# Local-global attention and a gated feed-forward on one core: the order of all steps as a written table, scores one pair of heads a stage

## The chip, the cores and the metric

The kernel runs on one core of a Trainium2 chip. The metric is device time in microseconds (us) of one execution. The core's engines each work through their own queue in order: TensorE (PE in the profile, its weight loads PEld), VectorE (DVE), ScalarE (ACT), GpSimd (POOL), and the sync engine (SP), whose queue here issues all loads and stores. An instruction whose inputs are not ready holds everything behind it in its queue.

## The reference, cut to what matters

```python
# batch 8, 8 heads, 512 local and 32 global positions, head size 64
k_all, v_all = concat(k_g, k_l), concat(v_g, v_l)
out_g = softmax(q_g @ k_all.T / 8) @ v_all                   # global rows see everything
s_ll = where(|i - j| <= 32, q_l @ k_l.T / 8, -1e9)           # local rows: a band of 32 ...
out_l = softmax(concat(q_l @ k_g.T / 8, s_ll)) @ v_all       # ... and the global keys
x = concat(out_g, out_l) with the heads side by side         # (8, 544, 512)
h = relu(x @ w_in)                                           # 512 -> 1024
c = conv over positions, three taps, each channel by itself, with conv_w
out = (h * sigmoid(c)) @ w_out                               # 1024 -> 512
```

The three weights of the feed-forward arrive as float64.

## The kernel before, in words

Everything is cut into short steps, named by a key and a number, and each step sends a few instructions to one engine.

*Attention.* Heads are taken in pairs (n = 0, 2, ..., 62; eight heads a batch). LQ, LK, LV and LG load queries, keys, values and global queries. S multiplies one pair's queries with its keys (64 small matmuls, L337) into one of two PSUM tiles, `four[0]` and `four[1]`. M (L370, DVE) adds the band mask and takes the minimum, E (L380, ACT) exponentiates with a sum, NS (L387, L388, DVE) inverts the sum, NP multiplies with it (L394 on ACT, L401 on POOL), DT (L409, DVE) transposes in blocks of 32. For four heads together, P (L433, 160 small matmuls) multiplies with the values into both `four` tiles. G, GM (L480), GE (L489), GN (L496, L497) and GS (L510 on POOL, L512 on DVE) do the same for the global rows; XG (L470) and GX (L518, a copy, L520) collect their outputs. XH0, XH1 (copies, ACT) and XL0, XL1 (L461, DVE) split the local outputs into a high and a low part, the tile `x`.

*Feed-forward.* A unit u is 128 of the 1024 hidden channels for one batch, eight units a batch (u = 0 to 63), and u = 64 to 71 for the global rows of all batches. Za and Zb (six matmuls of 512 columns each, L545) make it, RE is the relu (L558 on ACT), C1 (L321), Ca and Cb (L572, DVE) are the three taps; for two units together TH (L579, ACT) is the tanh of the sigmoid, GG (L583, DVE) the gate, GH (copy, ACT) and GL (L285) the high and low part. Oa to Od (six matmuls each, L603) make 128 of the 512 outputs of a batch (o = 0 to 35), OE copies them out, ST stores. Za needs both XL0 steps of its batch and Zb both XL1 steps, so the units of a batch start when both its P steps have been split.

*Weights.* WD loads one of eight pieces. WA (L145), WB (L150), WC (L155, L158), WH, WL (L161, L246), and WS and WX rebuild high and low parts from the float64 bits; i = 0 to 3 are `w_in`, 4 to 7 `w_out`. WT does the same for the taps (L150 to L195).

*The order.* A planner (`plan`, `arranged`) simulates the five engines with a table of costs and a due time for each step (POS, POS0, POS1, POS7), starts on each engine the ready step with the earliest due time, and the start times give the order in which `emit` writes the steps; instructions of one engine are then tied to that order. Which engine a step with a choice uses is set for batch 0 (`ENG0`), batch 1 (`ENG1`) and the rest (`ENG`):

```python
ENG = dict(XH0="a", XH1="a", XC="p", GC="a", GS="v", GX="v", NP="a", RE="a", C1="p", GH="a", GL="v", OE="v")
ENG1 = dict(ENG, OE="a")
ENG0 = dict(ENG, NP="p", GL="p", OE="a", GS="p", WA="a", WH="a", WX="a")
```

("a" is ACT, "v" DVE, "p" POOL.) From batch 1 on the scores of two pairs are one step (`JOINED_S = 1`): 128 matmuls, into both `four` tiles. Buffers that bound the order: four PSUM banks for Z, O and weight sums, the two `four` tiles, three query tiles, two value tiles, two `hb` tiles (relu output of two units each), two output tiles.

The steps on PE stand in this order at the start of before: WS.0 S.0 WS.1 S.2 S.4 WS.3 G.0 S.6 P.0 S.8(+10) G.8 P.4 Za.0 S.12(+14) WS.2 Zb.0 Za.1 P.8 Zb.1 Za.2. On DVE: WT.0 WC.0 WL.0 WC.1 WL.1 M.0 M.1 WC.3 NS.0 WL.3 M.2 M.3 M.4 M.5 NS.2 WC.6 GM.0 GM.1 NS.4 GN.0 GN.1 M.6 M.7 DT.0 DT.2 DT.1 DT.3 NS.6 DT.4 WL.6 XG.0 XL0.0 XL1.0 DT.5 DT.6 DT.7 M.8 M.9 M.10 WC.4 NS.8 M.11 WL.4 GM.2 GM.3 NS.10 GN.2 GS.8 GN.3 DT.8 XG.4 GX.0 WC.2 XL0.4 XL1.4 WL.2. The sequence of PE steps goes 72 times from the large matmuls (Z, O, WS) to the small ones (S, G, P) or back.

Of the kernel before, what the change touches and what calls it, by code (L numbers as in the profile page):

```python
# [52 lines left out]

# [10 lines left out]

# [3 lines left out]


def joined(n, since):  # L70

    return n // H >= since


def group(n, since):

    return (n // 4 * 4, n // 4 * 4 + 2) if joined(n, since) else (n,)
# [7 lines left out]
def attn_moe(ctx: ExitStack, tc: tile.TileContext, q_d, k_d, vw_d, qg_d, w_in_d, w_out_d, cw_d, out_d):  # L85
# [23 lines left out]

# [33 lines left out]
    def magnitude(w1, t):  # L143
        if ENGS[0]["WA"] == "a":
            nc.scalar.activation(out=f(t), in_=f(w1), func=AF.Abs)  # L145
        else:
            nc.vector.tensor_scalar(out=t, in0=w1, scalar1=0x7FFFFFFF, scalar2=None, op0=ALU.bitwise_and)
# [146 lines left out]


# [29 lines left out]
    def SC(n):  # L325

        for i, n in enumerate(group(n, JOINED_S)):
            q, chunk = heads[n]["q"], n // 2 % 4
# [1 line left out]
            for j in range(2):  # L330
                heads.setdefault(n + j, {})["s"] = four[side][:, j, :].rearrange("p (r x) -> p r x", r=NR)
            for r in range(NR):
                a = (5 * chunk + r) * SG
                for c in range(4):
                    for j in range(2):
                        rows = slice(j * D, (j + 1) * D)
                        nc.tensor.matmul(  # L337
                            heads[n + j]["s"][c * SG : (c + 1) * SG, r, :], lhsT=q[rows, c, r * SG : (r + 1) * SG],
                            rhs=keys[rows, c, a : a + P], start=True, stop=True,
                        )  # L340
# [297 lines left out]
LIMIT = dict(h=2, o=2)  # L638

ENG = dict(  # L640
    XH0="a", XH1="a", XC="p", GC="a", GS="v", GX="v", NP="a", RE="a", C1="p", GH="a", GL="v", OE="v",
)
ENG1 = dict(ENG, OE="a")
ENG0 = dict(ENG, NP="p", GL="p", OE="a", GS="p", WA="a", WH="a", WX="a")
ENGS = (ENG0, ENG1, ENG)

WENG = "pppppppp"

POS = dict(
    LQ=-1179.98, LK=-3410.21, LG=1302.26, LV=-1044.64, S=-1927.26, M=-1916.07, E=-935.04, NS=2891.3, NP=8253.39,  # L650
    DT=-2510.34, P=-1946.35, XH0=1800.87, XH1=-4498.84, XL0=2189.67, XL1=3093.6, XC=5534.43, G=-1339.63,
    GM=-3274.47, GE=-451.99, GS=2245.45, GN=26.63, GT=-36.81, GC=28, GR=-0.44, GP=47.15, XG=-348.91, GQ=-4.66,
    GX=5026.07, GY=-21.58, Za=1343.76, Zb=-2970.26, RE=-593.24, C1=3333.74, Ca=2145.9, Cb=-2645.65, TH=1498.45,
    GG=-2809.9, GH=-734.2, GL=-6125.32, Oa=1476.86, Ob=-1928.39, Oc=1677.17, Od=-912.14, OE=617.79, ST=951.33,
    WD=-36.77, WA=33.34, WB=-18.75, WC=6.7, WH=38.83, WL=26.89, WN=20.71, WS=61.46, WX=14.24, WT=67.84,
)
POS1 = dict(
    LQ=1801.42, LK=-2868.41, LG=-3799.69, LV=-472.71, S=2444.32, M=1149.47, E=-672.25, NS=-5513.89, NP=2844.69,
    DT=1050.29, P=-4401.47, XH0=1286.05, XH1=2015.12, XL0=-2118.02, XL1=-717.31, XC=216.22, G=-2968.21,
    GM=-6577.04, GE=-1509.99, GS=3918.06, GN=712.21, GT=-229.9, GC=0.84, GR=4.1, GP=-28.82, XG=-1414.41, GQ=-30.93,  # L660
    GX=5714.37, GY=43.7, Za=-2590.8, Zb=-4371.92, RE=3415.51, C1=-122.5, Ca=-335.52, Cb=2146.37, TH=-1163.25,
    GG=-2103.3, GH=-3088.62, GL=4104.62, Oa=-1516.5, Ob=1968.56, Oc=-140.95, Od=219.28, OE=1828.41, ST=-6497.37,
    WD=-22.76, WA=-48.75, WB=-114.27, WC=-13.6, WH=0.78, WL=36.32, WN=-36.15, WS=38.29, WX=36.81, WT=-5.41,
)
POS0 = dict(
    LQ=-16.41, LK=-2244.01, LG=-2092.66, LV=-1226.62, S=1696.13, M=-664.98, E=86.91, NS=4459.15, NP=-2141.79,
    DT=4976.67, P=1974.19, XH0=-2061.92, XH1=1997.55, XL0=998.26, XL1=1299.57, XC=-2968.56, G=-3718.28,
    GM=-2110.34, GE=-2428.29, GS=-3518.18, GN=1309.03, GT=97.28, GC=-3.17, GR=39.33, GP=23.89, XG=-1857.03,
    GQ=-22.35, GX=1016, GY=50.57, Za=-581.53, Zb=1607.5, RE=-4855.65, C1=1559.02, Ca=705.17, Cb=-2338.26, TH=-2415,
    GG=-1071.76, GH=-2120.18, GL=5170.42, Oa=-3178.86, Ob=73.19, Oc=2656.84, Od=-1298.34, OE=491.38, ST=-327.94,  # L670
    WD=78.19, WA=80.77, WB=36.03, WC=-4.08, WH=21.61, WL=52.37, WN=-25.74, WS=-1.32, WX=40.49, WT=1.93,
)

POS7 = dict(
    LQ=2645.41, LK=-880.16, LG=2823.5, LV=1027.03, S=1496.11, M=210.85, E=-1231.68, NS=2371.06, NP=-1797.04,
    DT=1559.96, P=864.56, XH0=-1384.4, XH1=632.04, XL0=302.77, XL1=-2816.76, XC=-2975, G=-2414.68, GM=-476.12,
    GE=-2919.87, GS=2467.17, GN=-2779.13, GT=-36.81, GC=28, GR=-0.44, GP=47.15, XG=4526.77, GQ=-4.66, GX=-370.08,
    GY=-21.58, Za=555.05, Zb=-2600.7, RE=4478.11, C1=3298.11, Ca=-6114.75, Cb=589.4, TH=5989.37, GG=4383.12,
    GH=204.2, GL=-2432.36, Oa=2107.51, Ob=-1249.42, Oc=-6742.44, Od=3984.32, OE=-1144.6, ST=-1401.11, WD=-36.77,
    WA=33.34, WB=-18.75, WC=6.7, WH=38.83, WL=26.89, WN=20.71, WS=61.46, WX=14.24, WT=67.84,  # L680
)

POSS = (POS0, POS1, POS, POS7)
POSS_NAMES = ("POS0", "POS1", "POS", "POS7")
PHASE = (0, 1, 2, 2, 2, 2, 2, 3, 3)

LATE = (2113.34, 2097.81, 2247.08)
WPOS = [-3504.56, -1841.02, 715.35, -15.71, 675.83, 1857.69, 482.76, 1530.63]
LAST_BATCH = 7
SUMMED = 1200, 6000  # L690

def cost(key, e, wide=True):


    def act(n, calls=1, src=190, more=0):
        one = src + n * 5 // 6 - 100 + more
        return one * calls, one * calls + 100

    def psum(n, calls=1):
        one = 150 + n * 102 // 100 - 77
        return one * calls, one * calls + 80

    def fast(n, calls=1):
        one = 150 + n * 52 // 100 - 77
        return one * calls, one * calls + 77

    def two(n):
        return 110 + n, 190 + n  # L710

    def pool2(n):
        return 150 + n * 22 // 10, 180 + n * 22 // 10

    def pool1(n, calls=1):
        return (180 + n * 107 // 100) * calls, (180 + n * 107 // 100) * calls + 30

    def pe(t, more=175):
        return t, t + more

    def dma(kb):
        return kb * 1024 // 320, kb * 1024 // 320 + 2000

    n = SL if wide else 8 * GV - 2
    if key in COPIES:
        n, from_psum = {"GH": (2 * n, 0), "OE": (n, 1)}.get(key, COPIES[key])
        if e == "a":
            return act(n, src=155 if from_psum else 190)
# [392 lines left out]
```

## Time and profile before

| what | value |
|---|---|
| device time, median of 3 runs | 536.71 us (534.94 to 536.86) |
| the profiled execution: time, span | 535.9 us, 534.1 us |
| PE busy | 491.1 us (92% of the span) |
| PEld busy | 400.6 us (75%) |
| DVE busy | 419.7 us (79%) |
| ACT busy | 333.2 us (62%) |
| POOL busy | 107.3 us (20%) |
| HBM read, written | 39.35 MB, 8.96 MB (90 GB/s over the span) |

The span runs from the first to the last instruction. Busy shares are means over the whole span, and the first 70 us and the rest behave differently, so the stretches have to be read apart.

### The profile page before, as it was taken

To read this page: it belongs to the slowest core of one execution; us is meant where nothing else is said; L and a number is where in the kernel's file an instruction comes from. 1 tells how busy PE (TensorE), PEld (TensorE's weight loads), DVE (VectorE), ACT (ScalarE), POOL (GpSimd) and SP (SyncE) were. 2 spreads that over 40 slices of the span, in tenths; PEclk is the share of its full clock that TensorE was granted. 3 is DMA by queue.
4 is the path that set the end of the run, shared out by engine and by line. 5 is a ranking of instruction groups with operands and counts; after the bars stand their busy time and mean duration, and the time that the engine had idled before them with its cause. 6 is when DMAs were issued, how large, how long until landed. Compare 5 with 4: busy or idle time off the path is not lost.

```text
span 534.1 us, 16508 instructions
## 1 busy us (share of the span) xinstructions
PE 491.1 (92%) x6752; PEld 400.6 (75%) x6752; DVE 419.7 (79%) x1263; ACT 333.2 (62%) x1016; POOL 107.3 (20%) x153
## 2 busy tenths in 40 slices
...
GB/s 334 412 311 172 170 133 130 128 114 80 120 70 100 67 111 71 112 152 52 78 95 134 70 81 92 129 71 22 70 41 22 22 21 22 20 20 41 40 37 46
DMA packets 32668, 53.56 MB, mean 100 GB/s; under 512 B 2384, under 2 KB 20304, under 8 KB 31568
## 3 DMA queue, kind: packets, MB, share of 16 engines
...
HBM read 39.35 MB, written 8.96 MB: 90 GB/s over the span
## 4 chain that ended last, share of the span: by engine, by line
PE 80%; DVE 13%; ACT 4%; issue 1%; DMA 1%; SPq 0%; DVEq 0%
PE ps_o L603 34%; PE ps_h L545 31%; PE four L433 8%; PE four L337 5%; DVE pt L370 2%; DVE t L572 2%; DVE pt L409 2%; DVE wt L158 1%; PE psw L261 1%; PE four L358 1%; DMA cwr<-cw 1%; ACT pt L380 1%; DVE pt L512 1%; DVE pg L480 1%; ACT pt L394 1%
## 5 line engine op out<-in xcount | busy, mean ns | idle before, releaser
L603 PE MATMUL ps_o<-g,w_out 128*128 128x512 f32 (+1 forms) x864 | 207.1, 380 | 0.0
L545 PE MATMUL ps_h<-x,w_in 128*128 128x512 f32 x768 | 197.9, 395 | 6.9 <-DVE x L461 4.4
L603 PEld LDWEIGHTS ps_o<-g,w_out 128*128 128x128 f32 x864 | 154.7, 188 | 31.3 <-issue 1.9
L545 PEld LDWEIGHTS ps_h<-x,w_in 128*128 128x128 f32 x768 | 142.7, 189 | 39.8 <-DVE x L461 5.1
L572 DVE SCALAR_TENSOR_TENSOR t<-hb,cw,t 128x512 f32<-128x512 f32 (+1 forms) x144 | 103.9, 741 | 32.9 <-POOL t L321 32.4
L321 POOL TENSOR_SCALAR t<-hb,cw 128x512 f32<-128x512 f32 (+1 forms) x72 | 57.8, 806 | 316.7 <-ACT hb L558 284.6
L380 ACT ACTIVATE pt<-pt,negm 128x128 f32<-128x128 f32 x256 | 99.1, 391 | 14.5 <-DVE negm L370 14.4
L558 ACT ACTIVATE hb<-ps_h 128x512 f32<-128x512 f32 (+1 forms) x72 | 41.4, 575 | 76.8 <-PE ps_h L545 71.5
L394 ACT ACTIVATE pt<-pt,sums 128x128 f32<-128x128 f32 x224 | 69.0, 400 | 1.0 <-DVE sums L387 1.0
L579 ACT ACTIVATE t<-t 128x1024 f32<-128x1024 f32 (+1 forms) x36 | 36.6, 1016 | 37.4 <-DVE t L572 37.3
L433 PE MATMUL four<-pt,vf 32*64 32x128 f32 (+3 forms) x2560 | 49.2, 295 | 10.5 <-DVE pt L409 3.8
L370 DVE CUSTOM_DVE_ANT_0 pt<-four,mask 128x128 f32<-128x128 f32 x256 | 55.6, 284 | 3.0 <-PE four L337 3.0
L433 PEld LDWEIGHTS four<-pt,vf 32*64 32x64 f32 x2560 | 44.6, 139 | 16.9 <-issue 10.4
L409 DVE STREAM_TRANSPOSE pt<-pt 128x608 f32<-128x608 f32 (+1 forms) x64 | 52.3, 853 | 1.6 <-ACT pt L394 1.6
L583 DVE SCALAR_TENSOR_TENSOR t<-t,hb 128x1024 f32<-128x1024 f32 (+1 forms) x36 | 42.2, 1174 | 12.4 <-ACT t L579 12.2
L380 ACT ACTIVATION_READ_ACCUMULATOR pt<-pt,negm 128x1 f32 x256 | 48.7, 190 | 0.0
L282 ACT CAST g<-t 128x1024 fp32r<-128x1024 f32 (+1 forms) x36 | 36.3, 1007 | 15.0 <-DVE t L583 10.9
L337 PE MATMUL four<-k,q 64*32 64x128 f32 x2048 | 37.7, 298 | 5.9 <-DVE pg L480 3.6
L285 DVE TENSOR_TENSOR g<-t,g 128x1024 fp32r<-128x1024 f32 (+1 forms) x32 | 36.9, 1154 | 6.5 <-ACT g L282 6.3
L337 PEld LDWEIGHTS four<-k,q 64*32 64x32 f32 x2048 | 32.4, 115 | 12.2 <-issue 4.1
L282 ACT CAST x<-four 128x384 fp32r<-128x384 f32 x64 | 19.4, 381 | 19.9 <-PE four L433 17.7
L282 DVE COPY o<-ps_o 128x512 f32<-128x512 f32 (+1 forms) x28 | 18.3, 654 | 14.0 <-PE ps_o L603 13.8
...
## 6 DMA issues: line engine op xcount, KB each, us to landing
vf<-vw SPq DMA_DIRECT2D x16, 640.0 KB, 4.2
q<-q SPq DMA_DIRECT2D x32, 256.0 KB, 4.0
out<-o SPq DMA_DIRECT2D x32, 256.0 KB, 2.1
...
```

Of the source, the lines that this page charges most:

```text
L282: nc.scalar.copy(out=out, in_=in_) if choice(key) == "a" else eng(key).tensor_copy(out=out, in_=in_)
L321: nc.gpsimd.tensor_scalar(out=out, in0=in_, scalar1=by, scalar2=0.0, op0=ALU.mult, op1=ALU.add)
L337: nc.tensor.matmul(heads[n + j]["s"][c * SG : (c + 1) * SG, r, :], lhsT=q[rows, c, r * SG : (r + 1) * SG], rhs=keys[rows, c, a : a + P], s ...
L370: nc.vector.tensor_tensor_reduce(out=out, in0=st["s"][:, r, :], in1=mask[:, v : v + 4].rearrange("p a c -> p (a c)"), op0=ALU.add, op1=ALU ...
L380: nc.scalar.activation(out=p, in_=p, func=AF.Exp, scale=-1.0, bias=st["m"][:, r : r + 1], accum_out=two["r"][:, n % 2, r : r + 1],)
L394: nc.scalar.activation(out=p, in_=p, func=AF.Copy, scale=by[:, r : r + 1])
L409: nc.vector.transpose(out=t, in_=t)
L433: nc.tensor.matmul(out, lhsT=vf[rows, j, s, :], rhs=pt, start=s == order[0], stop=s == order[-1])
L545: nc.tensor.matmul(hid[u]["z"], lhsT=w[:, ft, ct, :], rhs=x, start=ct + i == 0, stop=ct == NCT - 1 and i == 2)
L572: nc.vector.scalar_tensor_tensor(out=t, in0=rows_of(u, k)[:, u % 2], scalar=cw[:, 3 * ft + k : 3 * ft + k + 1], in1=t, op0=ALU.mult, op1=A ...
L583: nc.vector.scalar_tensor_tensor(out=t, in0=t, scalar=1.0, in1=rows_of(u, 1), op0=ALU.add, op1=ALU.mult)
L603: nc.tensor.matmul(ps, lhsT=w_out[w][:, mt, ft, :], rhs=g[:, k, ft % 2, :], start=ft + i == 0, stop=ft == NFT - 1 and i == 2,)
```

## The change: what it does

The planner is gone; the order is a table, `ORDER`, that `emit` walks through. Engines are set by `ENGINES`, and for single steps by `MOVED`. The scores of every pair are a step of their own, with the `four` tile given by `SIDES`. The taps' load is a step of its own (CW), their WT step is split (WTa on ACT) and two instructions shorter, and both stand later.

Counted over the table: 1471 steps for 1455 (14 more S, CW, WTa); PE goes 84 times between large and small matmuls. Steps with another engine than before: to ACT from POOL NP.1, 3, 5, 6, 7 and C1.0, 1, 3, 4, 5, 9, 10, 12, 15; to POOL from ACT NP.9, 10, 12, 13, 14; to POOL from DVE GS.8, 9, 12, 13, GX.0, GX.8, GL.9; to DVE from POOL WB.0, WB.2, GL.3, GL.7; to DVE from ACT RE.10, 11, 12 and OE.0, 1, 3, 6, 7. GL.1 and GL.5 stay on POOL.

The steps on PE at the start of after: S.0 S.2 WS.0 S.4 WS.1 G.0 S.6 WS.3 P.0 S.8 S.10 G.8 P.4 S.12 Za.0 S.14 Zb.0 WS.2 Za.1 Zb.1 Za.2 P.8. On DVE: WB.0 WC.0 WL.0 M.0 WC.1 M.2 M.1 WL.1 M.3 M.5 M.4 WC.3 NS.2 GM.0 GM.1 WL.3 NS.0 GN.1 M.7 GN.0 M.6 DT.3 DT.1 DT.2 DT.0 NS.4 WC.6 WL.6 XG.0 NS.6 XL1.0 XL0.0 DT.5 M.9 M.8 M.10 M.11 DT.7 WC.4 GM.3 DT.6 GM.2 DT.4 NS.10 WL.4 GN.3 WB.2 WC.2 XG.4 XL0.4 XL1.4 NS.8 GN.2 WT.0 WL.2. On SP: WD.0 LK.0 LG.0 LQ.0 WD.1 LQ.2 LK.2 LG.16 LK.6 LQ.6 LK.4 LQ.4 WD.3 LV.0 LV.4.

```diff
-    def rest(out, w0, w1, p, low):
-
-        v = nc.vector
-        v.tensor_scalar(out=w1, in0=w1, scalar1=low, scalar2=None, op0=ALU.bitwise_and)
-        v.scalar_tensor_tensor(out=f(w1), in0=w0, scalar=2.0**-32, in1=w1, op0=ALU.mult, op1=ALU.add)
-        v.scalar_tensor_tensor(out=out, in0=f(w1), scalar=2.0**-20, in1=f(p), op0=ALU.mult, op1=ALU.mult)
...
+    def CW(i):
+        nc.sync.dma_start(out=cwr.rearrange("p n w -> p (n w)"), in_=cw_d)
...
+    def WTa(i):
+        if wpe == 2:
+            magnitude(cwr[:, :, 1], cw.bitcast(U32))
...
-            magnitude(w1, t)
             clamped(t, nc.vector)
             scaled_bits(w1, t, 0x7FFFF8)
             power(cwp, t)
-            rest(f(cwp), w0, w1, cwp, 0)
+            nc.vector.scalar_tensor_tensor(
+                out=f(cwp), in0=w0, scalar=2.0**-52, in1=f(cwp), op0=ALU.mult, op1=ALU.mult
+            )
...
     def choice(key):
-        return ENGS[phase[0]][key]
+        for e, which in MOVED.get(key, {}).items():
+            if now[0] in which:
+                return e
+        return ENGINES[key]
...
     def SC(n):
 
-        for i, n in enumerate(group(n, JOINED_S)):
-            q, chunk = heads[n]["q"], n // 2 % 4
-            side = i if joined(n, JOINED_S) else SIDE["S", n]
+        q, chunk = heads[n]["q"], n // 2 % 4
+        for j in range(2):
+            heads.setdefault(n + j, {})["s"] = four[int(SIDES[n // 2])][:, j, :].rearrange("p (r x) -> p r x", r=NR)
...
-        nc.vector.tensor_tensor(out=t, in0=t, in1=gos[2 * b + 1], op=ALU.add)
+        eng("GX").tensor_tensor(out=t, in0=t, in1=gos[2 * b + 1], op=ALU.add)
         cp("GX", hi, t)
-        nc.vector.tensor_tensor(out=lo, in0=t, in1=f(hi), op=ALU.subtract)
+        eng("GX").tensor_tensor(out=lo, in0=t, in1=f(hi), op=ALU.subtract)
...
+MOVED = {
+    "C1": {"a": (0, 1, 3, 4, 5, 9, 10, 12, 15,)},
+    "GL": {"p": (1, 5, 9,)},
+    "GS": {"p": (0, 1, 4, 5, 8, 9, 12, 13,)},
+    "GX": {"p": (0, 8,)},
+    "NP": {"p": (0, 2, 4, 9, 10, 12, 13, 14,)},
+    "OE": {"a": (2, 4, 5,)},
+    "RE": {"v": (10, 11, 12,)},
+    "WB": {"v": (0, 2,)},
+}
...
+SIDES = "01001001010101101101101001010101"
...
+ORDER = """
+WD.0 LK.0 LG.0 LQ.0 WD.1 LQ.2 LK.2 WA.0 WB.0 LG.16 LK.6 S.0 WC.0 LQ.6 LK.4 WL.0 WH.0 LQ.4 WD.3 WA.1 LV.0 LV.4
+S.2 M.0 WB.1 WD.6 WD.2 E.0 WC.1 WS.0 M.2 WH.1 M.1 E.2 WL.1 S.4 WX.0 M.3 WA.3 WS.1 M.5 E.1 WB.3 M.4 WC.3 E.3 G.0
...
+Cb.68 Cb.69 Zb.70 TH.69 Oc.30 GG.69 GH.69 Za.71 RE.70 C1.70 Od.30 Ca.70 GL.69 Zb.71 OE.30 Od.31 Cb.70 RE.71
+C1.71 Ca.71 Oa.32 Cb.71 OE.31 TH.71 Ob.32 ST.31 GG.71 Oa.33 ST.30 GH.71 Oc.32 GL.71 Ob.33 Od.32 Oc.33 OE.32
+ST.32 Oa.34 Od.33 Ob.34 OE.33 ST.33 Oa.35 Ob.35 Oc.34 Oc.35 Od.34 Od.35 OE.34 ST.34 OE.35 ST.35
+"""
+def emit(tc, now, fns):
...
+    for step in ORDER.split():
+        key, i = step.split(".")
+        now[0] = int(i)
```

## Rows read from the trace of the kernel before

**Rows 1.** Busy time by stretch: stretch, its length, engines, PEclk, DMA share, GB/s.
```profile
6.20:68.50 62.30, 35.20 (x826) 24.18 (x827) 53.92 (x195) 45.22 (x148) 27.79 (x41) 0.79 0.83 280
68.50:140.00 71.50, 68.61 (x1127) 54.94 (x1126) 67.70 (x211) 58.18 (x186) 23.98 (x21) 0.96 0.42 113
...
140.00:482.00 342.00, 338.52 (x4504) 277.32 (x4503) 274.16 (x810) 216.61 (x662) 47.37 (x59) 1.00 0.23 71
482.00:534.10 52.10, 48.79 (x300) 44.15 (x298) 22.61 (x37) 11.14 (x19) 5.48 (x11) 1.00 0.11 42
```

**Rows 2.** Waits of PE from 82 us on: waiter, releaser, total us, times, longest.
```profile
PE ps_h L545 <- DVE x L461: 2.2, 1, 2.2
```

**Rows 3.** Timeline of PE around one joined score step: start, us, instruction group.
```profile
167.27 1.52 PE L545 MATMUL ps_h<-x,w_in 128*128 128x512 f32 x6
168.72 2.12 PE L337 MATMUL four<-k,q 64*32 64x128 f32 x128
170.76 1.66 PE L603 MATMUL ps_o<-g,w_out 128*128 128x512 f32 x6
...
173.64 1.52 PE L603 MATMUL ps_o<-g,w_out 128*128 128x512 f32 x6
```

**Rows 4.** Timeline of DVE up to the end of batch 0's `x`.
```profile
6.21 0.18 DVE L150 TENSOR_SCALAR cw<-cw 128x24 f32<-128x24 f32 x1 [2.70 <-ACT cw L145]
...
8.50 0.68 DVE L155 TENSOR_SCALAR wt<-wt 128x1024 uint32<-128x1024 uint32 x1
...
19.04 0.29 DVE L370 CUSTOM_DVE_ANT_0 pt<-four,mask 128x128 f32<-128x128 f32 x1 [1.90 <-PE four L337]
...
60.01 0.76 DVE L512 TENSOR_SCALAR pt<-pg,gnegm 128x32 f32<-128x32 f32 x4
...
60.95 0.79 DVE L409 STREAM_TRANSPOSE pt<-pt 128x608 f32<-128x608 f32 x1
...
64.03 0.73 DVE L518 TENSOR_TENSOR go<-go 128x128 f32<-128x128 f32 x1
...
65.26 0.69 DVE L155 TENSOR_SCALAR wt<-wt 128x1024 uint32<-128x1024 uint32 x1
...
67.12 1.41 DVE L461 TENSOR_TENSOR x<-four,x 128x384 fp32r<-128x384 f32 x4
```

**Rows 5.** Groups of DVE instructions between 6.2 and 68.5 us: count, busy us, mean ns, idle.
```profile
L388 DVE RECIPROCAL sums<-sums 128x8 f32<-128x8 f32 x6 | 1.2, 203 | 0.2
```

**Rows 6.** Groups of instructions over the whole span.
```profile
L285 DVE TENSOR_TENSOR g<-t,g 128x1024 fp32r<-128x1024 f32 (+1 forms) x32 | 36.9, 1154 | 6.5 <-ACT g L282 6.3
...
L282 DVE COPY o<-ps_o 128x512 f32<-128x512 f32 (+1 forms) x28 | 18.3, 654 | 14.0 <-PE ps_o L603 13.8
...
L401 POOL TENSOR_TENSOR pt<-pt,sums 128x128 f32<-128x128 f32 (+1 forms) x16 | 13.3, 857 | 6.2 <-ACT w_in L282 3.3 <-DVE sums L388 1.8 <-DVE gnegm L496 1.0
```

**Rows 7.** Timeline of DVE: the same four taps beside POOL's GL and without it.
```profile
107.29 4.87 DVE L572 SCALAR_TENSOR_TENSOR t<-hb,cw,t 128x512 f32<-128x512 f32 x4
...
125.49 2.73 DVE L572 SCALAR_TENSOR_TENSOR t<-hb,cw,t 128x512 f32<-128x512 f32 x4
```

**Rows 8.** Timeline of POOL: its first weight step, and one GL.
```profile
7.29 1.04 POOL L150 TENSOR_SCALAR wt<-wt 128x1024 f32<-128x1024 f32 x1 [3.88 <-ACT wt L145]
...
108.16 2.79 POOL L285 TENSOR_TENSOR g<-t,g 128x1024 fp32r<-128x1024 f32 x1 [6.37 <-ACT g L282]
```

**Rows 9.** The last matmuls on PE.
```profile
515.75 15.04 PE L603 MATMUL ps_o<-g,w_out 128*128 128x512 f32 x108
```

**Rows 10.** The last GL on DVE.
```profile
520.83 0.74 DVE L285 TENSOR_TENSOR g<-t,g 128x556 fp32r<-128x556 f32 x1 [0.73 <-ACT g L282]
```

**Rows 11.** DMA issues: count, KB each, median us from issue to landing.
```profile
vf<-vw SPq DMA_DIRECT2D x16, 640.0 KB, 4.2
q<-q SPq DMA_DIRECT2D x32, 256.0 KB, 4.0
```

More of the change, by code (lines that the diff above doesn't have):

```diff
@@ L1 @@
 from contextlib import ExitStack
-import heapq
 import numpy as np
@@ L67 @@
 FIRST, LAST = MASK.index("x0+0"), MASK.index("0-0x")
[L70 to L77, printed above, removed]
 def f(ap):
@@ L143, in magnitude @@
     def magnitude(w1, t):
[L144 to L147, printed above, removed]
+        nc.scalar.activation(out=f(t), in_=f(w1), func=AF.Abs)
     def clamped(t, e):
@@ L325, in SC @@
     def SC(n):
-        for i, n in enumerate(group(n, JOINED_S)):
-            q, chunk = heads[n]["q"], n // 2 % 4
-            side = i if joined(n, JOINED_S) else SIDE["S", n]
[L330 to L340, printed above, removed]
+        q, chunk = heads[n]["q"], n // 2 % 4
+        for j in range(2):
+            heads.setdefault(n + j, {})["s"] = four[int(SIDES[n // 2])][:, j, :].rearrange("p (r x) -> p r x", r=NR)
+        for r in range(NR):
+            a = (5 * chunk + r) * SG
+            for c in range(4):
+                for j in range(2):
+                    rows = slice(j * D, (j + 1) * D)
+                    nc.tensor.matmul(
+                        heads[n + j]["s"][c * SG : (c + 1) * SG, r, :], lhsT=q[rows, c, r * SG : (r + 1) * SG],
+                        rhs=keys[rows, c, a : a + P], start=True, stop=True,
+                    )
     def G(n):
@@ L615, in ST @@
         nc.sync.dma_start(out=out_d[:, a : a + n], in_=outs[o])
-    emit(tc, B, dict(
+    emit(tc, now, dict(
         LQ=LQ, LK=LK, LV=LV, XC=XC, LG=LG, G=G, S=SC, M=MA, E=EX, NS=NS, NP=NP, DT=DT, P=PV,
```

444 lines of the change are left out of this document (79 added, 365 removed).

## The prediction

> **What bounds the kernel now.** I read the busy time by stretch first [rows 1]. The reader is to see two kernels in it. From 140 to 482 us PE is busy 338.5 of 342.0 us at the full clock (granted share 1.00, the level of 2.4 GHz), and in the last 52.1 us it is busy 48.8. Nothing but PE's own work sets the time there: an order can win a few us at most, and can only lose by opening gaps. From 6.2 to 68.5 us it is the other way round: PE is busy 35.2 of 62.3 us and was granted 0.79 of its clock on average, so it spent part of that at the level of 1.2 GHz, while DVE is busy 53.9 of 62.3. Between 68.5 and 140 us both are nearly full, PE 68.6 and DVE 67.7 of 71.5.
>
> The waits of PE come second [rows 2]. After 82 us PE waits on DVE once, for 2.2 us, on an XL step. With the 2.9 us of idle time between 68.5 and 140 [rows 1], that is all a better order can take out behind the front.
>
> Third, the timeline of DVE in the front [rows 4]. The reader is to see what stands ahead of the first unit: DVE starts at 6.21 with the taps' weights, which nothing needs before the first unit's relu; its first score minimum stands at 19.04 behind a wait of 1.90 for the scores; batch 0's `x` is complete after the subtractions that begin at 67.12 and end at 68.5. From there PE is fed. So the time is the moment at which `x` of batch 0 is complete, plus PE's work, plus what PE waits later.
>
> **Part A: what stands ahead of the first unit.** I count DVE's queue up to XL1.4 in both orders; it is the fullest engine there, 53.9 us of work and 8.4 of waits [rows 1]. The table takes out of that queue:
> - WT, from 6.21 to 8.50: 2.3 us [rows 4].
> - GS.8 (now POOL), 60.01 to 60.69, its group of four: 0.76 at most, 0.7 taken; DT.8: 0.79; GX.0 (now POOL), 64.03 to 65.26: 1.2 [rows 4].
> - NS.8 and GN.2, four instructions of about 0.2 [rows 5]: 0.8.
>
> Together 5.8 us. It adds WB.0 and WB.2 on DVE. The trace has no WB on DVE; the nearest row is a tensor-scalar of the same 1024 columns, 0.69 [rows 4], and POOL's WB took 1.04 [rows 8]. So 0.7 each, 1.4 together (bounds 0 and 2.1). DVE's first step is now WB.0. In before POOL began the same step at 7.29 [rows 8], so DVE starts 1.1 us later than 6.21. In exchange, WB.0 hands nothing to another engine and back.
>
> The wait of 1.90 at 19.04 goes: S.0 was queued on PE behind the sums WS.0; in the table S.0 and S.2 stand first on PE, and their loads stand first on SP behind one weight piece. What is late next there is S.4 and G.0, behind WS.0 and WS.1, whose place I leave at no cost, since DVE has WL.1, M.3 and WC.3 to work on meanwhile. If that cover is too short, each costs DVE a wait like the 1.90 that went.
>
> A = -5.8 + 1.4 + 1.1 - 1.9 = -5.2 us for the first unit.
>
> **Part B: what comes back before 140 us.** Of A, WT, NS.8, GN.2 and DT.8 are only postponed: +3.9 us of DVE. Steps that leave DVE in this stretch: GS.9, 12 and 13 (0.7 each [rows 4]), GX.8 (1.2), GL.9 (1.15 [rows 6]): -4.4. Steps that come to DVE: GL.3 and GL.7, 2 x 1.15 = 2.3; RE.10 to 12 and OE.0, 1 and 3, six passes of 512 columns from PSUM. OE on DVE has a row, 0.65 [rows 6]; RE on DVE has none and the same size, so 6 x 0.65 = 3.9 (RE from 0 to twice that).
>
> One thing is freed. While POOL ran GL.3 for 2.79 us from 108.16 [rows 8], four taps on DVE took 4.87 us; the same four took 2.73 later [rows 7]. DVE lost 2.1 us. GL.3 and GL.7 leave POOL, so between 2.1 and 4.2 us of such holding go; I take 2.1, as only one has the row here.
>
> Sum on DVE: 3.9 - 4.4 + 6.2 - 2.1 = +3.6. So DVE's lead falls from 5.2 to 1.6 us if it was full, and DVE was idle 3.8 us of this stretch [rows 1], which an earlier start can fill: 1.6 to 5.4, or 7.5 with the second hold. PE's lead is between DVE's low end, 1.6, and 5.2 plus its own 2.9 us of gaps, 8.1. I take 5.5, a little above the middle: behind 82 us PE waited on DVE a single time [rows 2], so most of DVE's queue was not what PE waited for.
>
> **Part C: more changes between small and large matmuls.** The score step at 168.72 is 128 matmuls in 2.04 us. The six matmuls before it take 1.45 to the next start instead of 1.36, and the twelve behind it 2.88 instead of 2.72 [rows 3]. An excursion therefore costs 0.09 + 0.16 = 0.25 us beside its matmuls. The table goes 84 times between the kinds, 12 more, so 6 more excursions: +1.5 (bounds 0, where a gap would have been there anyway, and 1.5).
>
> **At no cost.** ACT gains five NP and nine C1, and loses five NP, three RE and three OE on DVE before 140 us: about 3 more passes of 0.65, and it has 13.3 us idle in that stretch [rows 1]; without that cover 2 us. Splitting S leaves its matmuls as they are. Loads: the shortest distances in the table are a query load (LQ.60), freed by S.56 and needed 5.1 us of PE work later, and a value load (LV.44) with four groups of 1.36, 5.4 us; they land after 4.0 and 4.2 [rows 11], 4.5 to 4.7 with SP's issue time. Hidden; if SP stands behind a store, each costs its excess, 1 to 2 us, and what is queued behind it on PE is the whole unit stream. ST.26 is issued two stores late; the other output tile covers it. At the end, one Od instead of two stands between Zb.71 and the last small outputs. Zb.71 ends at about 515.9 [rows 9], the last GL at 521.6 [rows 10], 5.7 us later, of which 0.6 was a copy (OE.30) that now stands earlier. The cover is 1.36 + 5 x 0.77 = 5.2 us against 5.1: nothing, or 0.6 if the copy is not what it waited for.
>
> **The sum.** -5.5 + 1.5 = -4.0 us. Against the profiled execution's 535.9 (span 534.1 and 1.8 around it) that is 531.9. The median of the runs shown is 536.71, 0.8 above the profiled one, which lies inside their range; I keep 531.9. Bounds: -8.1 with free excursions gives 527.8; -1.6 + 1.5 gives 535.8.
>
> **Rivals.**
>
> *The lead is given back on DVE.* The first unit starts 5 us earlier, but the postponed WT, the GL, RE and OE steps that came to DVE fill its queue between 70 and 140 us, PE waits for XL and GL steps there, and the excursions take the rest. The time is the low end of part B: 535.8. For it: DVE was busy 95% of that stretch. Against it: PE had almost no gap there. The change would then move the front without moving the end.
>
> *POOL holds DVE* (slower). NP.9, 10, 12, 13 and 14 go to POOL just where DVE is fullest, between 65 and 100 us. Each is two instructions of 0.857 [rows 6], 8.6 us in all. If DVE loses the share that it lost beside GL, 2.1 of 2.79 or 77% [rows 7, 8], that is 6.6 us more. DVE's lead of 1.6 becomes a delay of 5.0; with the excursions 535.9 + 5.0 + 1.5 = 542.4. It decides from a hold of about 2.8 us on (1.6 of lead less 1.5 of excursions leaves 0.1; 2.7 more is slower by 0.5%). For it: the row. Against it: eight NP were on POOL in before too, all in batch 0 [rows 6], and the wait that stood longest in DVE's queue there was one for PE [rows 4]; DVE work that reads PSUM or transposes need not be held. The Trainium skill states this rule: GPSIMD Engine Reference, section Key points, has GpSimd share its SBUF interfaces with VectorE, with contention for VectorE instructions of two SBUF inputs or in a two-port mode. The taps have two SBUF inputs, and the trace agrees, with 4.87 against 2.73.
>
> **How the numbers follow.** Forecast 0.60, lead given back 0.25, POOL holds DVE 0.15. What a measurement of this kernel can tell from no change is about 0.5%, 2.7 us: faster is below 534.0, slower above 539.4. The likeliest case has its own range of 527.8 to 534; the given-back lead lies within 0.5%, the last rival above. So faster 0.60, same 0.25, slower 0.15. For 8 times in 10 the range runs from 526.5, a little under the lower bound, as the waits of DVE in the front (8.4 us) could fall by more than 1.9, up to 539, which takes in the given-back lead and the milder part of the holding.
>
> **What would show it.** Part A: batch 0's last XL ends near 63.3 instead of 68.5; the first minimum is not preceded by a wait for scores; DVE's work ahead of it is shorter by WT, GS.8 and GX.0. Part B: PE busy between 68.5 and 140 stays above 66 us; GL.3 and GL.7 take 1.15 on DVE and the taps beside them keep 0.68 each. Part C: six more excursions at 0.25 each, and no new wait of PE behind 140 us. The prediction is wrong if PE shows waits for DVE between 70 and 140 us in sum above 3 us, if NP on POOL goes with stretched taps or gates, or if a load (LQ.28, LQ.60, LV.44) ends a wait of PE. It is wrong the other way if batch 0's last XL ends before 60 us and the units follow it without a gap.

## The result, and the profile after

The changed kernel takes 528.46 us (median of 4 runs, 528.16 to 529.19); the kernel before, run beside it, 536.08 (534.94 to 536.86). The ratio is 0.9862, with a 95% interval from 0.9838 to 0.9885: faster by 7.6 us. The profiled execution took 528.16 us, with a span of 526.4. The forecast was 531.9, a gain of 4.0. Sign and range held; the gain is almost twice as large.

Busy time by stretch, changed kernel (columns as in [rows 1]):

```profile
6.20:61.10 54.90, 31.41 (x856) 22.52 (x860) 49.71 (x177) 44.79 (x150) 18.18 (x33) 0.80 0.89 304
...
75.00:100.00 25.00, 25.00 (x520) 20.07 (x523) 24.10 (x75) 24.44 (x76) 9.84 (x13) 1.00 0.34 81
...
68.50:140.00 71.50, 70.54 (x1172) 56.26 (x1171) 68.23 (x197) 62.22 (x189) 23.15 (x28) 1.00 0.38 104
...
482.00:526.40 44.40, 40.67 (x259) 37.21 (x257) 19.98 (x34) 9.57 (x18) 5.21 (x9) 1.00 0.12 43
```

PE's share between 68.5 and 140 us rose from 68.6 [rows 1] to 70.5 of 71.5 us: it is full. What PE waits for from 82 us on, changed kernel:

```profile
PE four L410 <- issue: 1.5, 2, 0.8
PE ps_h L522 <- DVE go L447: 0.6, 1, 0.6
PE ps_h L522 <- DVE hb L537: 0.3, 1, 0.3
PE four L314 <- DVE x L438: 0.2, 1, 0.2
```

The 2.2 us behind an XL step [rows 2] are gone, and no load stands in the list, although the median value load now lands after 5.4 us and the median query load after 4.5, at or near the shortest distances in the prediction.

Timeline of DVE, changed kernel (answers to [rows 4], and to the taps of [rows 7]):

```profile
6.85 0.69 DVE L131 TENSOR_SCALAR wt<-wt 128x1024 f32<-128x1024 f32 x1 [3.34 <-ACT wt L128]
...
11.44 0.28 DVE L347 CUSTOM_DVE_ANT_0 pt<-four,mask 128x128 f32<-128x128 f32 x1
...
56.17 2.98 DVE L139 SCALAR_TENSOR_TENSOR wt<-raw,wt 128x1024 uint32<-128x1024 uint32 x1
...
59.08 0.61 DVE L447 TENSOR_REDUCE go<-four 128x64 f32<-128x192 f32 x2
59.61 1.54 DVE L438 TENSOR_TENSOR x<-four,x 128x384 fp32r<-128x384 f32 x4
...
81.12 1.34 DVE L560 SCALAR_TENSOR_TENSOR t<-t,hb 128x1024 f32<-128x1024 f32 x1
...
84.00 0.81 DVE L386 STREAM_TRANSPOSE pt<-pt 128x608 f32<-128x608 f32 x1
...
87.51 2.73 DVE L549 SCALAR_TENSOR_TENSOR t<-hb,cw,t 128x512 f32<-128x512 f32 x4
...
92.15 1.18 DVE L560 SCALAR_TENSOR_TENSOR t<-t,hb 128x1024 f32<-128x1024 f32 x1
```

DVE starts at 6.85 with WB.0, the first score minimum follows at 11.44 without a wait, and batch 0's `x` is complete at 59.61 + 1.54 = 61.15 us. Before it was 68.53. The later rows are read under the rivals.

To see where the gain is made I use a milestone in PE's queue: the start of P.20. Up to it both orders put the same work on PE (28 Z steps, 10 O, 12 S, 3 G, 4 WS, 5 P). On the timeline of PE it stands, in the kernel before and in the changed one, at

```profile
144.78 2.73 PE L433 MATMUL four<-pt,vf 32*64 32x96 f32 x159
```

```profile
135.76 2.75 PE L410 MATMUL four<-pt,vf 32*64 32x96 f32 x160
...
189.18 1.52 PE L580 MATMUL ps_o<-g,w_out 128*128 128x512 f32 x6
190.63 1.16 PE L314 MATMUL four<-k,q 64*32 64x128 f32 x64
191.72 1.67 PE L522 MATMUL ps_h<-x,w_in 128*128 128x512 f32 x6
193.23 2.91 PE L580 MATMUL ps_o<-g,w_out 128*128 128x512 f32 x12
```

| stretch | before | after | difference |
|---|---|---|---|
| start to `x` complete | 68.53 | 61.15 | -7.4 |
| `x` complete to P.20 | 76.25 | 74.61 | -1.6 |
| P.20 to the end | 389.3 | 390.6 | +1.3 |
| span | 534.1 | 526.4 | -7.7 |

Everything is won before 136 us, and a little is lost behind it. TensorE's clock does not make the difference: the mean granted share is 0.79 [rows 1] and 0.80 up to `x`, 0.97 in both kernels from `x` to P.20, and 1.00 (the level of 2.4 GHz) in both behind it.

### The profile page after: what moved, and what is told of

Its sections match the earlier page's. It is cut to its first block, busy times and chain, and to the rows that moved or that the text cites. A ratio compares the mean times of both kernels' runs of the same rounds, so it can differ in the third digit from the quotient of the medians.

```text
span 526.4 us, 16468 instructions
## 1 busy us (share of the span) xinstructions
PE 490.3 (93%) x6752; PEld 398.3 (76%) x6752; DVE 416.8 (79%) x1252; ACT 334.3 (64%) x1017; POOL 100.1 (19%) x161
## 4 chain that ended last, share of the span: by engine, by line
PE 81%; DVE 9%; ACT 4%; DMA 3%; issue 2%; POOL 1%; SPq 0%; ACTq 0%
PE ps_o L580 34%; PE ps_h L522 33%; PE four L410 7%; PE four L314 6%; DMA raw<-w_in 2%; DVE pt L386 1%; DVE pt L347 1%; PE four L335 1%; DVE t L549 1%; ACT pt L357 1%; DMA q<-q 1%; DVE pt L489 1%; DVE x L438 1%; POOL pt L487 1%; ACT x L263 0%
## 5 line engine op out<-in xcount | busy, mean ns | idle before, releaser
L300 POOL TENSOR_SCALAR t<-hb,cw 128x512 f32<-128x512 f32 (+1 forms) x63 | 51.6, 824 | 330.2 <-ACT hb L535 173.1
L535 ACT ACTIVATE hb<-ps_h 128x512 f32<-128x512 f32 (+1 forms) x69 | 39.2, 569 | 62.6 <-PE ps_h L522 60.9
L347 DVE CUSTOM_DVE_ANT_0 pt<-four,mask 128x128 f32<-128x128 f32 x256 | 56.9, 284 | 5.7 <-PE four L314 5.7
L314 PE MATMUL four<-k,q 64*32 64x128 f32 x2048 | 40.3, 302 | 19.7 <-DMA q<-q 7.9
L410 PE MATMUL four<-pt,vf 32*64 32x128 f32 (+3 forms) x2560 | 46.1, 286 | 9.7 <-DVE sums L364 4.1
L410 PEld LDWEIGHTS four<-pt,vf 32*64 32x64 f32 x2560 | 42.2, 134 | 16.7 <-issue 11.3
L266 DVE TENSOR_TENSOR g<-t,g 128x1024 fp32r<-128x1024 f32 (+1 forms) x33 | 38.5, 1169 | 11.1 <-ACT g L263 11.0
L263 DVE COPY o<-ps_o 128x512 f32<-128x512 f32 (+1 forms) x33 | 21.6, 655 | 15.4 <-PE ps_o L580 15.3
```

The source lines that it names most:

```text
L263: nc.scalar.copy(out=out, in_=in_) if choice(key) == "a" else eng(key).tensor_copy(out=out, in_=in_)
L300: nc.gpsimd.tensor_scalar(out=out, in0=in_, scalar1=by, scalar2=0.0, op0=ALU.mult, op1=ALU.add)
L314: nc.tensor.matmul(heads[n + j]["s"][c * SG : (c + 1) * SG, r, :], lhsT=q[rows, c, r * SG : (r + 1) * SG], rhs=keys[rows, c, a : a + P], s ...
L347: nc.vector.tensor_tensor_reduce(out=out, in0=st["s"][:, r, :], in1=mask[:, v : v + 4].rearrange("p a c -> p (a c)"), op0=ALU.add, op1=ALU ...
L410: nc.tensor.matmul(out, lhsT=vf[rows, j, s, :], rhs=pt, start=s == order[0], stop=s == order[-1])
```

## The experiments

Twelve kernels were run. Each stands here with the end of batch 0's `x`, the start of P.20 and the span of its profiled execution, then the median and the ratio to the kernel before, run beside it (median 535.9 for the first four, 536.5 for the next four, 536.6 for the last four). These medians of one kernel differ by up to 0.7 us, so a difference of that size between kernels of different fours is not told from none.

| kernel | `x` | P.20 | span | median | ratio, 95% interval |
|---|---|---|---|---|---|
| front only | 61.83 | 139.90 | 528.4 | 530.15 | 0.9892 [0.9875, 0.9909] |
| rest only | 67.87 | 142.17 | 533.2 | 534.92 | 0.9984 [0.9971, 0.9998] |
| engines of before | 62.05 | 144.01 | 534.2 | 536.48 | 1.0015 [0.9994, 1.0037] |
| scores joined | 61.54 | 135.02 | 525.1 | 526.72 | 0.9825 [0.9807, 0.9843] |
| NP back on ACT | 60.44 | 139.01 | 530.5 | 531.63 | 0.9904 [0.9880, 0.9929] |
| only NP moved | 62.76 | 142.90 | 534.5 | 535.18 | 0.9985 [0.9963, 1.0006] |
| only the engines | 69.73 | 145.24 | 535.2 | 535.41 | 0.9979 [0.9965, 0.9994] |
| joined, WC.2 later | 60.54 | 135.92 | 526.5 | 528.39 | 0.9855 [0.9833, 0.9876] |
| RE, OE back on ACT | 61.34 | 136.28 | 527.4 | 528.70 | 0.9852 [0.9840, 0.9865] |
| C1, GL back on POOL | 61.70 | 139.78 | 530.2 | 531.99 | 0.9911 [0.9898, 0.9925] |
| taps first | 61.45 | 136.16 | 526.3 | 528.04 | 0.9842 [0.9825, 0.9858] |
| WS.0 first | 66.17 | 140.42 | 531.3 | 531.70 | 0.9903 [0.9884, 0.9923] |

The column P.20 carries most of the table: in the kernels that have the changed order behind it, 390.1 to 391.6 us follow that start; where the order of before stands there it is 389.3 (the kernel before), 388.5 ("front only") and 390.0 ("only the engines").

**Which half, order or engines.** The first theory, "front", was the prediction's: the time is the moment of `x`, and what comes behind keeps the lead. Two hybrids switch at XL1.4: one has the changed order and engines up to it and those of before behind it, the other the reverse. Their `ORDER` at the seam:

```diff
-XH1.4 XL0.4 GS.9 WX.3 XL1.4 S.12 NS.8 NP.11 GN.2 Za.0 WT.0 WH.2
+XH1.4 XL0.4 GS.9 WX.3 XL1.4 WT.0 WX.1 XC.0 NS.8 LQ.16 NP.8 LG.24 GN.2
...
-WX.4 XL0.4 WH.2 XL1.4 Za.0 WL.2 S.12 S.14
+WX.4 XL0.4 WH.2 XL1.4 LQ.20 GS.9 S.12 Za.0 S.14 WL.2 Zb.0
```

> The new table up to the step XL1.4 (batch 0's x complete), with its engines; every later step in the order and on the engines of the kernel before, joined scores included. Theory 1, the gain is made in the front: x of batch 0 stands 7.4 us earlier than in before (61.1 for 68.5 us), PE is fed from there and the rest is neutral, so about 528.5 us (527 to 530.5). Rival, the later order and engines are needed to keep the lead, since DVE was 95% busy there in before: 532 to 536 us.

> The reverse: the order and engines of the kernel before up to XL1.4, every later step as in the new table. Theory 1 (front): the lead is missing, 535 us, less at most the 2.9 us of PE gaps that before had between 68.5 and 140 us: 532.5 to 536.5. Rival (the rest of the table carries the gain): 530 us or less.

The front alone is worth 5.8 us, the rest alone 1; both times lie in the ranges of "front". The third kernel keeps the whole changed order and takes every engine from before; a fourth does the opposite:

```diff
 MOVED = {
-    "C1": {"a": (0, 1, 3, 4, 5, 9, 10, 12, 15,)},
-    "GL": {"p": (1, 5, 9,)},
-    "GS": {"p": (0, 1, 4, 5, 8, 9, 12, 13,)},
-    "GX": {"p": (0, 8,)},
-    "NP": {"p": (0, 2, 4, 9, 10, 12, 13, 14,)},
-    "OE": {"a": (2, 4, 5,)},
-    "RE": {"v": (10, 11, 12,)},
-    "WB": {"v": (0, 2,)},
+    "GL": {"p": (1, 3, 5, 7,)},
+    "GS": {"p": (0, 1, 4, 5,)},
+    "NP": {"p": (0, 1, 2, 3, 4, 5, 6, 7,)},
+    "OE": {"a": (0, 1, 2, 3, 4, 5, 6, 7,)},
```

> The new order unchanged, but every step on the engine that it had before (all of C1 on POOL, NP of batch 0 on POOL and of batch 1 on ACT, GS.8 to 13 and GX on DVE, GL.3 and GL.7 on POOL, OE of batches 0 and 1 on ACT). Theory order: the gain is the order's, the engines cost 1 to 3 us, as five DVE steps come back near XL1.4 and two GL go back beside DVE: 529.5 to 531.5 us. Rival, the per-step engines carry it: 534 us or more.

> The other half of the change alone: the order of the kernel before, every step on the engine that the new table gives it. Theory: engines and order were laid out for each other, and the front of the old order (taps first, scores behind WS.0) keeps batch 0's x at about 67 us; gain of at most 2 us: 534 to 537 us. Rival, the engines carry the gain by themselves: 531 us or less.

Here "front" fell. With the engines of before, `x` is complete at 62.05, only 0.9 later than in the changed kernel, and yet the whole gain, 8.0 us (536.48 against 528.46), is gone. Engines alone are worth about 1 us. Neither order nor engines pays by itself ("front only" kept its 5.8 with order and engines of before behind the seam, which belong together), so I went on with a second theory: order and engines are a pair, and the lead at `x` is kept only if the queues of ACT, DVE and POOL between 68 and 140 us fit it. Of that stretch, the longest waits of PE and DVE in the kernel with the engines of before:

```profile
102.06 1.66 PE L522 MATMUL ps_h<-x,w_in 128*128 128x512 f32 x6 [3.05 <-ACT hb L535]
```

```profile
104.00 1.18 DVE L136 TENSOR_SCALAR wt<-wt 128x1024 uint32<-128x1024 uint32 x1 [2.64 <-POOL wt L131]
...
134.85 2.09 DVE L549 SCALAR_TENSOR_TENSOR t<-hb,cw,t 128x512 f32<-128x512 f32 x2 [3.52 <-POOL t L300]
```

PE waits for a relu of ACT, DVE for a weight step and for taps of POOL. In the changed kernel PE waits for no relu of ACT in that stretch, and DVE's two waits for POOL are 0.2 us each.

**Which engine move.** Three kernels undo one group each in the changed kernel, and one does the first group alone on top of the engines of before:

```diff
-    "NP": {"p": (0, 2, 4, 9, 10, 12, 13, 14,)},
+    "NP": {"p": (0, 2, 4,)},
...
-    "C1": {"a": (0, 1, 3, 4, 5, 9, 10, 12, 15,)},
-    "GL": {"p": (1, 5, 9,)},
+    "GL": {"p": (1, 3, 5, 7, 9,)},
...
-    "OE": {"a": (2, 4, 5,)},
-    "RE": {"v": (10, 11, 12,)},
+    "OE": {"a": (0, 1, 2, 3, 4, 5, 6, 7,)},
```

> The changed kernel with one group of engine moves undone: NP.9, 10, 12, 13 and 14 (batch 1's weights times 1/sum) on ACT again. Theory ACT: in the changed kernel ACT is busy 19.4 of the 20 us from 80 to 100 us, so 5 x 1.2 us more of NP there delay the splits XH and relus RE that PE waits for; 4 to 6 us slower than the changed kernel, 532.5 to 534.5 us, while POOL's hold on DVE beside NP.10 (1.75 us) goes. Rival, POOL's hold costs more than ACT's time: 527 us.

> The new order with the engines of the kernel before (536.5 us) except one group: NP.9, 10, 12, 13 and 14 on POOL as in the changed kernel. Theory ACT: this group makes most of the difference between 536.5 and 528.5 us, 530 to 532 us. Rival, the other moves (C1 to ACT, GL.3 and GL.7, RE and OE to DVE, GS and GX to POOL) make it: 534 us or more.

> The changed kernel with the nine moved C1 (C1.0, 1, 3, 4, 5, 9, 10, 12, 15) and GL.3 and GL.7 back on GpSimd, the order kept. Theory (order and engines are a matched pair): C1 stands behind NP on POOL between 75 and 145 us, the taps, the gates and their second output buffer come later, PE waits; P.20 starts 2 to 4 us later than 135.8, 530 to 533. By the prediction's price alone (two GL holds of 2.1 come back on DVE, less 2 x 1.15 that leave it): +1.9 at most, 528.5 to 530.4, with four taps beside a GL on POOL at 4.5 to 4.9 us. Rival (POOL has time for them, PE does not wait): 527.8 to 528.8.

> The changed kernel with RE.10 to 12 and OE.0, 1, 3, 6 and 7 back on ScalarE, the order kept. Theory (order and engines are a matched pair): these steps are queued on ACT between the start of P.16 and 150 us, where the table counted on DVE for them; P.20 starts 1 to 3 us later than the 135.8 us of the changed kernel, and the time is that start plus 390 to 391.5: 529 to 531.5. Rival (only the places of NP and C1 matter, ACT has idle time there): P.20 within 0.5 us of 135.8, 527.8 to 528.8. Third (DVE is the bound there, as part B of the prediction priced it): eight passes of 0.65 leave DVE, P.20 starts earlier, 526 to 527.5.

*NP.* With the five NP on ACT, `x` is complete 0.7 us earlier, but P.20 and the time are 3.2 later. Stretch by engine, one wait of PE, and NP on ACT, in that kernel:

```profile
75.00:100.00 25.00, 21.78 (x328) 16.74 (x310) 21.71 (x70) 24.81 (x78) 6.70 (x7) 0.96 0.35 81
```

```profile
98.56 2.93 PE L522 MATMUL ps_h<-x,w_in 128*128 128x512 f32 x6 [2.78 <-ACT hb L535]
```

```profile
79.92 1.26 ACT L371 ACTIVATE pt<-pt,sums 128x128 f32<-128x128 f32 x4
```

ACT is busy 24.8 of 25.0 us, and PE waits 2.78 us for a relu. The row of ACT is one NP, four instructions in 1.26 us, so the five are 6.3 us; between 75 and 100 us NP take 5.1 us of ACT, 1.3 in the changed kernel. What the end loses is less than that: from `x` to P.20 PE stands idle 3.5 us, for 0.3 in the changed kernel. In the latter ACT is full too between 75 and 100 us (24.44 of 25.00, first fence), but without these 3.8 us of NP. The expected 4 to 6 us were too many. ACT was also full in the same stage of the kernel before, from 13.9 us behind its `x` on:

```profile
82.40:107.40 25.00, 25.00 (x420) 20.18 (x419) 23.83 (x81) 24.06 (x83) 8.71 (x9) 1.00 0.56 147
```

*C1 and GL.* Undoing them costs 3.5 us, P.20 moves by 4.0. DVE and POOL in that kernel:

```profile
76.64 1.18 DVE L549 SCALAR_TENSOR_TENSOR t<-hb,cw,t 128x512 f32<-128x512 f32 x1 [1.24 <-POOL t L300]
...
100.36 0.69 DVE L136 TENSOR_SCALAR wt<-wt 128x1024 uint32<-128x1024 uint32 x1 [2.66 <-POOL wt L131]
...
130.86 1.90 DVE L549 SCALAR_TENSOR_TENSOR t<-hb,cw,t 128x512 f32<-128x512 f32 x2 [2.38 <-POOL t L300]
```

```profile
75.92 1.36 POOL L300 TENSOR_SCALAR t<-hb,cw 128x512 f32<-128x512 f32 x2
...
96.92 2.40 POOL L266 TENSOR_TENSOR g<-t,g 128x1024 fp32r<-128x1024 f32 x1 [3.16 <-ACT g L263]
99.29 1.04 POOL L131 TENSOR_SCALAR wt<-wt 128x1024 f32<-128x1024 f32 x1
...
127.62 2.40 POOL L266 TENSOR_TENSOR g<-t,g 128x1024 fp32r<-128x1024 f32 x1 [9.46 <-ACT g L263]
```

DVE waits 1.24 us for the first tap on POOL, 2.66 us for the weight step WB.5, which stands behind GL.3 in POOL's queue, and 2.38 us for a tap that stands behind GL.7: 6.3 us, where the changed kernel has 0.4. PE feels part of it: of P.20's 4.0 us, 0.6 are there at `x`, 2.0 are more idle time of PE and 1.4 more busy time (75.70 us instead of 74.28). The waits come from the order of POOL's queue, not from a hold of DVE's instructions, which run at their usual length but for one (WC.5 at 101.09, 1.52 us instead of 1.23 beside a C1). The expectation's four stretched taps did not come.

*RE and OE.* Undoing them costs nothing that can be told (+0.2 by the median). All eight passes stand behind the start of P.16; P.20 starts 0.5 later, with a wait of 0.8 us of PE for a relu of ACT. So the passes that stand ahead of P.20 were no burden on DVE that PE felt, and little relief for ACT.

The three groups sum to 3.2 + 3.5 + 0.2 = 6.9 of the 8.0. The other moves (NP.1, 3, 5, 6, 7, GS, GX, GL.9, WB) were not undone by themselves. Nor do the shares simply add: done alone on top of the engines of before, NP's move brings only 1.3, and DVE still waits 6.2 us for POOL (3.5 for a tap, 2.7 for WB.5). That expectation missed. It fits two queues in a row, of which each move frees one.

**What made the front shorter.** Two kernels undo one step each of the order:

```diff
-WD.0 LK.0 LG.0 LQ.0 WD.1 LQ.2 LK.2 WA.0 WB.0
+WD.0 CW.0 LK.0 LG.0 LQ.0 WD.1 LQ.2 LK.2 WTa.0 WT.0 WA.0 WB.0
...
-LG.16 LK.6 S.0 WC.0 LQ.6 LK.4 WL.0 WH.0 LQ.4 WD.3 WA.1 LV.0 LV.4 S.2 M.0 WB.1 WD.6 WD.2 E.0 WC.1 WS.0
+LG.16 LK.6 WC.0 LQ.6 LK.4 WL.0 WH.0 WS.0 S.0 LQ.4 WD.3 WA.1 LV.0 LV.4 S.2 M.0 WB.1 WD.6 WD.2 E.0 WC.1
```

> The changed kernel with the taps' load as the second load and WTa and WT ahead of the first weight step, as before; WT stays two instructions shorter. The prediction priced the later WT at 2.3 us of the 5.2 in the front. By that price batch 0's x is complete at 63.4 instead of 61.1 and the time is 530.8. By the trace of the changed kernel WT takes 1.2 us: x at 61.7 to 62.4, 529.0 to 529.8. Rival (DVE waits there for the first weight piece anyway, 3.3 us, and WT fits into that wait): x within 0.3 us of 61.1, 528.2 to 528.8.

> The changed kernel with the first weight sums (WS.0) ahead of the first scores on TensorE, as before. The first score minimum on DVE (M.0) then waits for weight work of DVE and ACT and for WS.0: a wait of 2 to 7 us on DVE at about 12 to 19 us, where the changed kernel has none. Theory (what DVE waits in the front decides when x is complete): x of batch 0 1.9 us (the wait of before) to 5 us later, 530.4 to 533.5. Rival (DVE catches up, since later waits in the front shrink by as much): x within 1 us of 61.1, 528.2 to 529.5.

DVE with the taps first, and DVE with WS.0 first:

```profile
6.54 0.18 DVE L131 TENSOR_SCALAR cw<-cw 128x24 f32<-128x24 f32 x1 [3.02 <-ACT cw L128]
...
7.71 0.69 DVE L131 TENSOR_SCALAR wt<-wt 128x1024 f32<-128x1024 f32 x1
```

```profile
16.92 0.29 DVE L347 CUSTOM_DVE_ANT_0 pt<-four,mask 128x128 f32<-128x128 f32 x1 [5.00 <-PE four L314]
```

The taps take 1.17 us, most of it in time in which DVE would wait for the first weight piece anyway: `x` moves by 0.3 us, the time not at all (the rival). WS.0 first costs DVE a wait of 5.00 us; `x` is 5.0 later, P.20 4.7, the median 3.2 (529.26 to 533.09, a wider spread than that of the others). The lead is thus mainly that scores come first.

**Splitting the scores, and a faster version.** One kernel puts five of the split pairs of S side by side again, by moving what stood between them:

```diff
-Za.0 WT.0 WH.2 WX.4 S.14
+WT.0 WH.2 WX.4 S.14 Za.0
...
-Za.4 LQ.22 M.16 RE.3 GL.1 DT.12 E.16 S.18
+LQ.22 M.16 RE.3 GL.1 DT.12 E.16 S.18 Za.4
...
-S.60 Ca.46
+S.60 S.62 Ca.46
```

(Likewise Zb.8 behind S.22, and Od.10 and Za.29 behind S.42.)

> The new table with five of its six split score stages brought together on PE (S.12 and 14, 16 and 18, 20 and 22, 40 and 42, 60 and 62), so five excursions between large and small matmuls fewer. Theory excursion: 5 x 0.25 = 1.25 us less, 527.2 us. Rival, the matmuls between the two halves cover the wait for the second PSUM tile (XL1): no gain, or up to 2 us more, 528.5 to 530.5 us.

It runs in 526.72 us (526.03 to 527.14, no overlap with the changed kernel's runs), 1.7 less (the intervals of the two ratios just touch), and beats both kernels. The rows of PE above give the price: from 190.63 to 191.72 us one pair takes 1.09 us, where a joined pair of steps takes 2.04 [rows 3], so a split pair costs 2 x 1.09 - 2.04 = 0.14 beside the 0.25 of the excursion, 0.39 together. Measured: 0.35 for each of the five by the medians, 0.26 by the spans; so 0.39 is an estimate, and good to about 0.1.

The last kernel adds one more edit to it, WC.2 behind XL1.4, to take the long instruction at 56.17 out of the way of `x`:

```diff
-WB.2 WC.2 WS.4 NP.10 XH0.4 XG.4 LV.12 XH1.4 XL0.4 GS.9 WX.3 XL1.4 S.12
+WB.2 WS.4 NP.10 XH0.4 XG.4 LV.12 XH1.4 XL0.4 GS.9 WX.3 XL1.4 WC.2 S.12
```

> The new table with the five score stages joined (526.7 us), and WC.2 moved on DVE from ahead of XG.4 to behind XL1.4. In the changed kernel one instruction of WC.2 takes 2.98 us for 1.23 beside POOL's NP.10, and XG.4 and XL0.4 stand behind it though P.4 ends at 56.8 us. Theory front: x of batch 0 is complete 1.5 to 2 us earlier and the end follows, 524.7 to 525.5 us. Rival, WC.2's 2 us come back behind it, and WS.2 or DVE's full queue takes the lead again: 526.5 to 527.5 us.

`x` comes 1.0 earlier, P.20 0.9 later, and the time is 1.7 longer, beyond the ranges of theory and rival. From `x` to P.20 PE is idle 2.9 us instead of 1.3, most of it in waits for DVE. An earlier `x` is worth nothing here, where DVE's work is only pushed behind it.

## Why the prediction was right, and where its sizes were wrong

**Part A: right mechanism, mis-sized waits.** `x` came 7.4 us earlier instead of 5.2. DVE's work ahead of it fell as priced, from 53.92 [rows 1] to 49.71: -4.2, for -4.4. Its waits from 6.2 us on fell from 8.38 to 54.90 - 49.71 = 5.19, by 3.2, where the terms +1.1 and -1.9 gave 0.8. Two single terms were off. WT was priced at 2.3; put back (in its shorter form, 1.17 us) it costs 0.3, since DVE has a wait there. "The wait of 1.90 goes" was read from a queue in which weight steps stood ahead of the minimum; put back in the new order it is 5.00. What was left out beside it is a wait of DVE in the kernel before that also went:

```profile
63.37 0.62 DVE L470 TENSOR_REDUCE go<-four 128x64 f32<-128x192 f32 x2 [1.63 <-PE four L433]
```

The same step, at 59.08 in the changed kernel, has no wait.

**Part B: the value taken was too low.** It took 5.5 us of lead, between 1.6 and 8.1. At P.20 the lead is 9.0: the whole 7.4, and PE's gaps besides, which is the case of the upper bound. The 3.9 us for RE and OE on DVE were no cost: of the six passes counted only four start ahead of 140 us (three RE, one OE), and without them on DVE P.20 comes no earlier, but 0.5 us later. GL.3 and GL.7 gave something back, but as POOL's queue, not as a hold.

**Part C: 0.25 was the excursion without the fixed part of a score step.** With 0.39, six excursions are 2.3 instead of 1.5. Three of them lie behind P.20, by that price 1.2 of the 1.3 us that are lost there; in the kernel with joined scores, where two of the three are gone, that stretch is 0.6 shorter. PE's waits between `x` and P.20 fell by 2.6: 2.16 [rows 2] and 0.73 before, 0.32 after. The second of them, kernel before:

```profile
PE ps_h L545 <- ACT hb L558: 0.7, 1, 0.7
```

The sum by stretches is then -7.4 at `x`, -2.6 of waits, +2.3, together -7.7, as measured. It leaves out two pieces that nearly cancel: behind P.20 PE is idle 0.7 us less, and from `x` to the end its busy time grew by 2.9 us instead of 2.3.

**"At no cost": the step that failed.** It covered ACT's moves with 13.3 us of idle time, a mean over 71.5 us. In the 25 us that matter ACT had 1 us idle. Undoing NP's move costs 3.2 us, undoing C1's and GL's 3.5. PE paid for both. The forecast came out right because the table had moved just these steps off the queues that PE and DVE would have waited for, which is luck and no term of the sum; its terms for changed engines nearly cancel (-1.9 + 1.4 in part A; -4.4 + 2.3 + 3.9 - 2.1 in part B, -0.8 in all), so by them the order with the engines of before would take about 532.7, and it runs in 536.48. Loads and the tail were indeed free: from 82 us on PE waits for no load, and in the last stretch it is idle 3.7 us, for 3.3 before [rows 1].

**The rivals.** *The lead is given back* did not happen (`x` to P.20 is shorter), but it is what the engines of before would have brought, through the queues of ACT and POOL and not through DVE's own work: there DVE is busy 70.7 us from `x` to P.20, for 70.4 in the changed kernel. *POOL holds DVE* happened once in the changed kernel: WC.2 at 56.17 takes 2.98 us instead of 1.23, beside

```profile
56.46 1.50 POOL L378 TENSOR_TENSOR pt<-pt,sums 128x384 f32<-128x384 f32 x2
57.63 2.54 POOL L487 TENSOR_SCALAR pt<-pg,gnegm 128x32 f32<-128x32 f32 x4
...
80.20 1.18 POOL L378 TENSOR_TENSOR pt<-pt,sums 128x128 f32<-128x128 f32 x2 [5.01 <-DVE sums L365]
...
83.62 2.39 POOL L266 TENSOR_TENSOR g<-t,g 128x1024 fp32r<-128x1024 f32 x1
```

That is 1.75 us, under the 2.8 from which the rival decides, and NP is worth more on POOL than it takes: with NP on ACT the instruction is 1.23 again and the kernel slower. The Trainium skill (GPSIMD Engine Reference, section Key points) names VectorE instructions of two SBUF inputs among those that contend with GpSimd. The trace agrees for WC.2. Elsewhere it was small: the gate at 81.12, beside the end of the NP instructions at 80.20 and the start of the next, takes 1.34 instead of the 1.18 of the next one (92.15), and the taps at 87.51, with no two-input step of POOL beside them, keep 2.73.

What stays open: why "front only" takes 78.1 us from `x` to P.20, 3.5 more than the changed kernel, was not taken apart further, as that seam fits neither order. Its largest pieces are a wait of 3.8 us of PE for a weight copy of ACT and one of 2.2 us for an XL step. In that kernel four taps beside a GL on POOL take 4.87 us again, as in the kernel before [rows 7].
